# Gating unit 0 alone, and moving the decay rows and the output stores to other DMA issuers, in a fused gated-recurrence and feed-forward kernel

## The chip, the cores and the metric

The kernel runs on one core of a Trainium2 chip. The metric is the device time of one execution in microseconds (us). Where two kernels are compared, a ratio with a 95% interval is given; how it is computed is said with the result. Time points in the text ("at 64.3") count from the first instruction of the profiled execution.

## The reference, cut to what matters

```python
# q, k, v, a_re, a_im: (4 batch, 8 heads, 768 steps, 48), float32
mag   = sqrt(a_re**2 + a_im**2)
scale = minimum(mag, 0.999) / (mag + 1e-6)       # a = (a_re + i a_im) * scale
for t in range(S):                               # S is a complex 48x48 state per head
    S = a[t][:, None] * S + outer(k[t], v[t])
    y[t] = q[t] @ real(S)
x = y as (3072 tokens, 384)
out = x + sigmoid(x @ w_res) * ((gelu(x @ w_gate) * (x @ w_val)) @ w_out)   # 384 -> 1536 -> 384
```

The kernel does not step through time. It takes 256 steps of one batch as a *group* (12 groups, two chunks of 128 steps each), and two groups as a *unit* (6 units, numbered 0 to 5). Within a group the products of decays become exponentials of cumulative sums of log|a| (tiles `E`, `Ei`) and sines of cumulative angles (`fg`, then `CS`), and attention runs on TensorE. Between groups a 96x384 state `G` is carried and multiplied by a decay `M`. `M` comes from rows that lie along one partition and are needed down the partitions: they are turned by writing them to DRAM and reading them back element by element. I call these the turned rows. A *ring* below is the DMA queue of one issuing engine. A *completion semaphore* is a counter that a DMA raises when it has landed and on which other instructions wait.

## The kernel before: what the change and the argument touch

ScalarE needs three function tables in turn: logarithm and exponential (the gate of the next unit), arctangent and sine, and Gelu (the feed-forward). So the work goes in phases. Phase X of unit u holds the rest of its attention, the exponentials of unit u+1, the logarithms of unit u+2 and the sines; phase Y holds the feed-forward of unit u and the first attention of unit u+1.

```python
    def load_q(g):
        for nm, src in (("q", q), ("k", k)):
            ...                                            # nc.sync.dma_start, one per chunk
        t = ldv.tile([128, C, H, D], BF, tag="v", name="v")
        for c in range(C):
            nc.gpsimd.dma_start(out=t[:, c], in_=rows(v, g, c))
    ...
    def turn(nm, g, srcs):                                 # rows to DRAM and back, turned
        n = len(srcs)
        md = dr.tile([n, DM], FP, tag="d" + nm, name="d" + nm)
        for i, src in enumerate(srcs):
            nc.gpsimd.dma_start(out=md[i:i + 1, :], in_=src)
        m = mp.tile([128, n, H], FP, tag=nm, name=nm)
        for u in range(2):
            nc.gpsimd.dma_start(out=m[u * D:(u + 1) * D].rearrange("p r h -> p (r h)"),
                                in_=md.rearrange("r (h d) -> d (r h)", h=H))
        T[nm, g] = m
    ...
    def decay3(g):                                         # M, placed behind the sines
        m = T["m2", g]
        M = mp.tile([128, H], FP, tag="M", name="M")
        nc.vector.tensor_tensor(out=M[0:DD], in0=m[0:DD, 0], in1=m[0:DD, 1], op=OP.mult)
        nc.vector.tensor_tensor(out=M[0:DD], in0=M[0:DD], in1=T["m1", g][0:DD, 0], op=OP.mult)
    ...
        def enter():                                       # attention of a group, first step
            ...
            nc.vector.tensor_tensor(out=G[0:DD], in0=G[0:DD], in1=Mb, op=OP.mult)   # needs M
    ...
    # cs_t: the folding of the angles that the sines need
        r = pS.tile([128, H, D], FP, tag="r", name="r")
        nc.vector.tensor_scalar(out=r, in0=cs3, scalar1=MAGIC, scalar2=MAGIC, op0=OP.add, op1=OP.subtract)
        nc.vector.tensor_tensor(out=fg[:, hs, 1, :], in0=cs3, in1=r, op=OP.subtract)
    ...
    # start: a of units 0 and 1 first, and both are gated in the first phase
    for g in gs(0) + gs(1):
        load_a(g)
    for g in gs(0):
        load_q(g)
    after_landing(T["k", 0], load_w_in)
    ...
        nc.sync.dma_start(out=out[t0:t0 + 128, :], in_=ot)
```

A scheduler orders each engine's instructions from the program's order and priorities. Each engine runs its own list in order.

## Time and profile before

The median was 344.27 us in three runs (342.91 to 344.88); the profiled execution spans 341.4 us.

| part of the span | us | what bounds it |
|---|---|---|
| start to the load of the first Gelu table | 0 to 94.0 | loads, ScalarE's chain, waits for turned rows |
| four units, Gelu table to Gelu table | 94.0 to 278.6 (46.8, 46.4, 47.3, 44.0) | TensorE |
| last unit and the end | 278.6 to 341.4 | TensorE |

The next lines are from the timeline of ScalarE, kernel before. In all views ACT is ScalarE, DVE VectorE, PE TensorE, POOL GpSimd and SP SyncE; a q behind the name marks a DMA that the engine only issues. The columns are start, duration, engine, source line, operation, output<-input, shapes and count; the brackets give how long the engine stood idle before it and what released it. A line with `x2` holds two instructions.

```profile
25.18 0.84 ACT L119 ACTIVATE ar<-ar 128x768 f32<-128x768 f32 x1
29.41 0.84 ACT L119 ACTIVATE ar<-ar 128x768 f32<-128x768 f32 x1 [3.38 <-DMA ar<-in_a_re_dram]
...
35.30 1.28 ACT L445 ACT_TABLE_LOAD   x1
...
64.32 0.21 ACT L119 ACTIVATE m_268<-m_268 96x8 f32<-96x8 f32 x1 [8.90 <-DMA m_268<-dm_266]
...
94.02 1.28 ACT L445 ACT_TABLE_LOAD   x1
...
95.90 1.08 ACT L119 ACTIVATE h_776<-gp 128x512 bf16<-128x512 f32 x2
```

Unit 0's exponentials are done at 25.2, but its trigonometric table is loaded only at 35.3, because unit 1's logarithms stand between. Later ScalarE stops 8.9 us for a turned row. The first Gelu is at 95.9. From there a unit takes about 46 us.

VectorE too stops once for a turned row, as its view of waits shows (line waited on, releaser, total us, times, longest):

```profile
DVE M L273 <- DMA m_247<-dm_244: 4.2, 1, 4.2
```

### The profile page before, as it was taken

To read this page: it belongs to the slowest core of one execution; us is meant where nothing else is said; L and a number is where in the kernel's file an instruction comes from. 1 tells how busy PE (TensorE), PEld (TensorE's weight loads), DVE (VectorE), ACT (ScalarE), POOL (GpSimd) and SP (SyncE) were. 2 spreads that over 40 slices of the span, in tenths; PEclk is the share of its full clock that TensorE was granted. 3 is DMA by queue.
4 is the path that set the end of the run, shared out by engine and by line. 5 is a ranking of instruction groups with operands and counts; after the bars stand their busy time and mean duration, and the time that the engine had idled before them with its cause. 6 is when DMAs were issued, how large, how long until landed. Compare 5 with 4: busy or idle time off the path is not lost.

```text
span 341.4 us, 5552 instructions
## 1 busy us (share of the span) xinstructions
PE 267.3 (78%) x2054; PEld 160.6 (47%) x2080; DVE 245.4 (72%) x440; ACT 203.0 (59%) x338; POOL 67.1 (20%) x104
## 2 busy tenths in 40 slices
PE   0330544298689979899897999779999989999995
PEld 0110224275256545465554566445665556565452
DVE  1322696249999649999389998499994799855443
ACT  3365434349665696756896656977568275662530
POOL 9423710050522224102232000150001300000000
PEclk9996585559699999999999999999999999999999
DMA  9999999999999999527422620021000210002002
GB/s 139 136 139 175 176 184 196 175 170 171 155 167 162 169 133 172 109 46 72 25 63 54 118 46 2 2 48 47 3 2 1 50 46 2 0 2 92 2 1 92
DMA packets 135258, 30.25 MB, mean 89 GB/s; under 512 B 127168, under 2 KB 135232, under 8 KB 135232
## 3 DMA queue, kind: packets, MB, share of 16 engines
q1 hardware_dynamic: 103296, 23.60, 40.6%
q0 software_dynamic: 31936, 6.31, 21.9%
q8 instruction: 16, 0.26, 0.3%
q14 instruction: 10, 0.08, 0.1%
HBM read 31.33 MB, written 4.76 MB: 106 GB/s over the span
## 4 chain that ended last, share of the span: by engine, by line
PE 47%; DMA 18%; DVE 15%; ACT 9%; issue 7%; POOL 3%; ACTq 0%; DVEq 0%; POOLq 0%
PE vp L414 12%; PE gp L410 11%; PE op L434 6%; DMA dm_266<-ar 4%; DMA v<-in_v_dram 4%; PE tp L320 3%; PE at L327 3%; PE tp L317 3%; PE rp L426 3%; DMA dm_663<-Ei 2%; ACT L445 2%; DVE fg L237 2%; DVE r L234 2%; DMA dm_219<-ar 2%; ACT CS L119 2%
## 5 line engine op out<-in xcount | busy, mean ns | idle before, releaser
L410 PE MATMUL gp<-xT,wg 128*128 128x512 bf16 x196 | 61.5, 382 | 7.6 <-DVE xT L401 4.6
L414 PE MATMUL vp<-xT,wv 128*128 128x512 bf16 x210 | 60.3, 382 | 0.3
L322 ACT COPY qk<-tp 96x512 bf16<-96x512 bf16 x48 | 27.9, 581 | 28.3 <-PE tp L320 15.1
L180 DVE TENSOR_TENSOR ai<-s,ai 128x768 f32<-128x768 f32 x12 | 11.1, 955 | 38.5 <-ACT s L119 26.9
L330 DVE TENSOR_TENSOR atm<-at,mask_81 128x512 bf16<-128x512 f32 x48 | 32.8, 683 | 7.2 <-PE at L327 7.2
L410 PEld LDWEIGHTS <-wg 128*128 128x128 bf16 x216 | 20.0, 98 | 23.0 <-issue 8.9
L317 PE MATMUL tp<-ident,Q 128*96 128x128 bf16 x192 | 20.1, 231 | 13.4 <-DVE qk L323 8.6
L142 POOL DMA_DIRECT2D v<-in_v_dram x24 | 21.3, 902 | 43.0 <-PE y L367 22.4
L414 PEld LDWEIGHTS <-wv 128*128 128x128 bf16 x216 | 20.4, 98 | 19.3 <-issue 0.8
L317 PEld LDWEIGHTS <-Q 128*96 128x96 bf16 x192 | 17.3, 131 | 21.4 <-issue 10.0
L323 DVE COPY qk<-tp 96x512 bf16<-96x512 bf16 x48 | 19.9, 414 | 10.1 <-ACT qk L322 9.6
L203 PE MATMUL csl<-ar,lt0a 128*128 128x384 f32 x24 | 12.3, 601 | 18.6 <-DVE ar L189 18.5
L119 ACT ACTIVATE CS<-fg,hpi 128x768 bf16<-128x768 f32 x12 | 11.2, 935 | 24.1 <-DVE fg L237 24.1
L445 ACT ACT_TABLE_LOAD x18 | 23.1, 1283 | 1.0 <-PEq L547 0.7
L320 PE MATMUL tp<-ident,K 128*96 128x128 bf16 x192 | 22.1, 235 | 0.0
L227 PE MATMUL cst<-ai,lt0b 128*128 128x384 f32 x24 | 11.6, 568 | 13.4 <-ACT ai L119 13.1
L327 PE MATMUL at<-qk 96*128 96x128 bf16 x192 | 20.4, 228 | 0.1
L437 DVE SCALAR_TENSOR_TENSOR ot<-sg,op 128x384 f32<-128x384 f32 x24 | 13.2, 549 | 9.4 <-PE op L434 9.4
L365 PE MATMUL y<-v,atm 128*128 128x48 bf16 x192 | 17.9, 187 | 2.5 <-DVE atm L330 2.4
L365 PEld LDWEIGHTS <-atm 128*128 128x128 bf16 x192 | 13.5, 98 | 12.8 <-DVE atm L330 11.6
L320 PEld LDWEIGHTS <-K 128*96 128x96 bf16 x192 | 17.3, 133 | 0.0
L357 PEld LDWEIGHTS <-K 128*96 128x96 bf16 x160 | 13.3, 138 | 6.5 <-DVE K L292 4.2
(155 smaller groups left out, 626.3 us busy)
## 6 DMA issues: line engine op xcount, KB each, us to landing
ar<-in_a_re_dram SPq DMA_DIRECT2D x24, 192.0 KB, 5.7
ai<-in_a_im_dram SPq DMA_DIRECT2D x24, 192.0 KB, 5.5
q<-in_q_dram SPq DMA_DIRECT2D x24, 192.0 KB, 5.1
k<-in_k_dram SPq DMA_DIRECT2D x24, 192.0 KB, 5.0
out_dram<-ot SPq DMA_DIRECT2D x24, 192.0 KB, 1.9
v<-in_v_dram POOLq DMA_DIRECT2D x24, 96.0 KB, 6.3
wg<-in_moe_w_gate_dram POOLq DMA_DIRECT2D x4, 288.0 KB, 9.2
wv<-in_moe_w_val_dram POOLq DMA_DIRECT2D x4, 288.0 KB, 10.5
```

The source lines that it names most:

```text
L142: nc.gpsimd.dma_start(out=t[:, c], in_=rows(v, g, c))
L317: nc.tensor.transpose(out=tp[0:DD, j * 128:j * 128 + 128], in_=Q(x), identity=ident)
L320: nc.tensor.transpose(out=tp[0:DD, 512 + j * 128:640 + j * 128], in_=K(x), identity=ident)
L322: nc.scalar.copy(out=qk[0:DD, 0:512], in_=tp[0:DD, 0:512])
L323: nc.vector.tensor_copy(out=qk[0:DD, 512:1024], in_=tp[0:DD, 512:1024])
L327: nc.tensor.matmul(out=at[:, j], lhsT=qk[0:DD, 512 + j * 128:640 + j * 128], rhs=qk[0:DD, j * 128:j * 128 + 128], start=True, stop=True)
L330: nc.vector.tensor_tensor(out=atm, in0=at, in1=mask4, op=OP.mult)
L365: nc.tensor.matmul(out=ys, lhsT=st["atm", hg][:, j], rhs=V(h), start=True, stop=first)
L410: nc.tensor.matmul(out=gp, lhsT=wg[:, fi, ffi * 128:(ffi + 1) * 128], rhs=xT[:, fi, :], start=(fi == 0), stop=(fi == KD - 1))
L414: nc.tensor.matmul(out=vp, lhsT=wv[:, fi, ffi * 128:(ffi + 1) * 128], rhs=xT[:, fi, :], start=(fi == 0), stop=(fi == KD - 1))
L434: nc.tensor.matmul(out=ps, lhsT=h2[:, ffi, jj * 128:(jj + 1) * 128], rhs=wo[:, ffi, :], start=(ffi == 0), stop=(ffi == KF - 1))
L445: tab(nc.scalar.preload_act_table_set(nm))
```

## The change

The intent: unit 0 is gated alone, so that its sines and its attention come sooner; unit 1's logarithms move into the next phase. q, k and v of unit 0 are loaded ahead of unit 1's a. The turned rows leave GpSimd's DMA queue, in which they stood behind weights, for a queue of ScalarE's own; three rows go in one turn, and `M` is computed on GpSimd. In exchange GpSimd issues the output stores.

```diff
+    def decay_rows(g):
+        er = pS.tile([1, DM], FP, tag="r", name="er")
+        act(out=er, in_=T["lm", g][0:1, 0:DM], func=AF.Exp)
+        md = dr.tile([3, DM], FP, tag="md", name="md")
+        for i, src in enumerate((T["E", g - 1][127:128, DM:W], T["Ei", g][0:1, 0:DM], er)):
+            nc.scalar.dma_start(out=md[i:i + 1, :], in_=src)
+    def decay(g):
+        m = mp.tile([128, 3, H], FP, tag="m", name="m")
         for u in range(2):
-            nc.gpsimd.dma_start(...)
+            nc.scalar.dma_start(out=m[u * D:(u + 1) * D].rearrange("p r h -> p (r h)"),
+                                in_=T["md", g].rearrange("r (h d) -> d (r h)", h=H))
         M = mp.tile([128, H], FP, tag="M", name="M")
-        nc.vector.tensor_tensor(out=M[0:DD], ...)                  # two of them
+        nc.gpsimd.tensor_tensor(out=M[0:DD], ...)                  # two of them
...
-        nc.sync.dma_start(out=out[t0:t0 + 128, :], in_=ot)
+        nc.gpsimd.dma_start(out=out[t0:t0 + 128, :], in_=ot)
...      # phase_x, u < 0: p1 of unit 0 only, then rows, table, arctangent, decay, fold, sines
+        if u == 0:
+            first = [st for g in g1 for st in p1_steps(g)]
+            weave((0.0, 0.3, first), (0.3, 0.4, csls), (0.4, 0.6, exs), (0.4, 0.7, p1),
+                  (0.7, 0.75, [trig] + [call(p1_arctan, g) for g in g1]), (0.72, 0.72, dec), (0.75, 0.9, cst),
+                  (0.9, 1.0, sin + atn), (0.0, 0.8, att))
+            return
...
-    for g in gs(0) + gs(1):
+    for g in gs(0):
         load_a(g)
     for g in gs(0):
         load_q(g)
-    after_landing(T["k", 0], load_w_in)
+        load_v(g)
+    for g in gs(1):
+        load_a(g)
+    after_landing(T["ai", 2], load_w_in)
+    for g in gs(1):
+        load_q(g)
...      # u == -1
-            for g in gs(1):
-                load_q(g)
-            after_landing(T["k", 2], load_w_out)
+            after_landing(T["q", 2], lambda: [load_v(g) for g in gs(1)])
+            after_landing(T["q", 3], load_w_out)
```

More of the change, by code (lines that the diff above doesn't have):

```diff
@@ L139, in load_q, with load_v @@
             T[nm, g] = t
+    def load_v(g):
         t = ldv.tile([128, C, H, D], BF, tag="v", name="v")
@@ L245, in p2_sin @@
         act(out=T["CS", g][:, :, 1], in_=T["fg", g][:, :, 1], func=AF.Sin, scale=2.0 * math.pi)
-    def turn(nm, g, srcs):
-        n = len(srcs)
-        md = dr.tile([n, DM], FP, tag="d" + nm, name="d" + nm)
-        for i, src in enumerate(srcs):
-            nc.gpsimd.dma_start(out=md[i:i + 1, :], in_=src)
-        m = mp.tile([128, n, H], FP, tag=nm, name=nm)
-        for u in range(2):
-            nc.gpsimd.dma_start(out=m[u * D:(u + 1) * D].rearrange("p r h -> p (r h)"),
-                                in_=md.rearrange("r (h d) -> d (r h)", h=H))
-        T[nm, g] = m
-    def decay0(g):
-        turn("m1", g, [T["lm", g][0:1, 0:DM]])
-    def decay1(g):
-        m = T["m1", g]
-        act(out=m[0:DD], in_=m[0:DD], func=AF.Exp)
-    def decay2(g):
-        turn("m2", g, [T["E", g - 1][127:128, DM:W], T["Ei", g][0:1, 0:DM]])
-    def decay3(g):
-        m = T["m2", g]
+    def decay_rows(g):
[4 more added lines that the diff above has]
+            nc.scalar.dma_start(out=md[i:i + 1, :], in_=src)
+        T["md", g] = md
+    def decay(g):
+        m = mp.tile([128, 3, H], FP, tag="m", name="m")
+        for u in range(2):
+            nc.scalar.dma_start(out=m[u * D:(u + 1) * D].rearrange("p r h -> p (r h)"),
+                                in_=T["md", g].rearrange("r (h d) -> d (r h)", h=H))
         M = mp.tile([128, H], FP, tag="M", name="M")
-        nc.vector.tensor_tensor(out=M[0:DD], in0=m[0:DD, 0], in1=m[0:DD, 1], op=OP.mult)
-        nc.vector.tensor_tensor(out=M[0:DD], in0=M[0:DD], in1=T["m1", g][0:DD, 0], op=OP.mult)
+        nc.gpsimd.tensor_tensor(out=M[0:DD], in0=m[0:DD, 0], in1=m[0:DD, 1], op=OP.mult)
+        nc.gpsimd.tensor_tensor(out=M[0:DD], in0=M[0:DD], in1=m[0:DD, 2], op=OP.mult)
         T["M", g] = M
@@ L472, in phase_x @@
         d1 = [g for g in g1 if g % NS > 0]
-        d2 = [g for g in g2 if g % NS > 0]
         ops = [call(op_step, u - 1, jj) for jj in range(4)] if 0 <= u - 1 < NU else []
@@ L484, in ex @@
             pend.pop(0)()
-        def p1(g):
-            return p1_steps(g) + ([call(decay0, g)] if g % NS > 0 else [])
         csls = [call(csl, g, c) for g in g1 for c in range(C)]
-        exs = [ex for _ in g1 for _ in range(C)]
-        dec = [call(decay2, g) for g in d1]
-        atn = [table("trig_and_small")] + [call(p1_arctan, g) for g in g2]
+        exs = [ex for _ in g1 for _ in range(C)] + [call(decay_rows, g) for g in d1]
+        dec = [call(decay, g) for g in d1]
         cst = [call(carry, g) for g in g1] + [call(cs_t, g, c) for g in g1 for c in range(C)]
         sin = [call(p2_sin, g) for g in g1]
-        dec1 = [call(decay1, g) for g in d1]
-        dec3 = [call(decay3, g) for g in d1]
+        trig = table("trig_and_small")
         table("natural_log_exp_and_others")()
         if u < 0:
-            for f in [st for g in g1 for st in p1(g)] + csls + exs + dec + zip_steps([p1(g) for g in g2]) + dec1:
-                f()
-            for f in atn[:1] + [call(p1_arctan, g) for g in g1] + cst + sin + atn[1:] + dec3:
+            for f in ([st for g in g1 for st in p1_steps(g)] + csls + exs + [trig]
+                      + [call(p1_arctan, g) for g in g1] + dec + cst + sin):
                 f()
             return
-        weave((0.0, 0.12, csls), (0.05, 0.5, zip_steps([p1(g) for g in g2])), (0.01, 0.01, dec1), (0.12, 0.45, exs),
-              (0.46, 0.46, dec), (0.2, 0.65, cst), (0.7, 0.95, atn + sin), (0.95, 0.95, dec3), (0.0, 0.8, att), (0.1, 1.0, ops))
+        atn = [call(p1_arctan, g) for g in g2]
+        p1 = zip_steps([p1_steps(g) for g in g2])
+        if u == 0:
[4 more added lines that the diff above has]
+            return
+        weave((0.0, 0.12, csls), (0.05, 0.5, p1), (0.12, 0.45, exs), (0.46, 0.46, dec), (0.2, 0.65, cst),
+              (0.7, 0.95, [trig] + atn + sin), (0.0, 0.8, att), (0.1, 1.0, ops))
     def phase_y(u):
@@ L532 @@
             load_q(g)
+            load_v(g)
 _INS = ['q', 'k', 'v', 'a_re', 'a_im', 'moe_w_gate', 'moe_w_val', 'moe_w_out', 'moe_w_res']
```

## The prediction

> **What bounds the kernel now.** From 96 us on, the timeline shows a steady 46 us per unit (feed-forwards start at about 96, 142, 188, 234, 280). There TensorE is busy 41 of 46 us at full granted clock (table by windows): near a compute floor, 245 of the 341.4 us. The first 96 us are start-up: TensorE is busy about 42 us, often at half clock, and the page's DMA row is full. Unit 0's exponentials are ready at 25.2 us, but its arctangent starts at 36.6: in between ScalarE waits for and works on unit 1's a. Attention starts at 48.2; at 55.4 ScalarE stops for 8.9 us for a turned decay row (waits view: m_268), because that row took 13.9 us in GpSimd's queue behind the weights. VectorE waits 4.2 us for another (m_247).
>
> **What the change does.**
> 1. Unit 0 is gated alone and its q, k, v come ahead of unit 1's a; 4 instead of 12 v loads compete at the start. ai of group 1, awaited until 17.1 us, should land at 13 to 16. The trigonometric table load comes at about 24 instead of 35.3, attention at 32 to 37 instead of 48.
> 2. The 8.9 and 4.2 us waits for turned rows go.
> 3. Unit 1's first pass is not removed, it moves into the next phase. I count about 43 us of ScalarE work between unit 0's first sine and the first Gelu; if ScalarE is 80 to 90% busy, the first Gelu comes at 78 to 87 us instead of 96. DMA can bind here: unit 2's a now comes behind unit 1's q and k and beside the weights; from the trace's rates (one 192 KB load per us alone, half that beside weights) it lands near 60 us, just in time or some us late.
> 4. Given back: ScalarE gets, per decay (8), a one-row exponential (0.49 us), three small DMA issues and two of 1,152 elements. SyncE needs 0.5 us to issue 1,024 rows when quiet; I estimate 2 us of ScalarE per decay, plus waits for the round trip. In the gate phases ScalarE is packed until its second table load, then idles 2 to 3 us for VectorE; so 2 to 4 us in all, 8 if its issues block.
> 5. Stores by GpSimd: 0.5 to 0.9 us per issue in the trace, against 0.36 on SyncE, on an idle engine; about 1 us at the tail. The Trainium skill ("DMA: Bandwidth & Descriptors", Issuing engines are not separate dma queues) says all issuing engines share the same 16 DMA engines; so I expect the own ring to cure the queueing of item 2, not to add bandwidth. The trace agrees: loads slow down beside weights.
>
> **Critical path and time.** Start-up gains 9 to 18 us, about 15; items 4 and 5 take back about 4. Predicted 333 us, range 326 to 341. Chances: faster 0.76, same 0.20, slower 0.04.
>
> **What would show it.** Step 1: table load near 24 us, first attention matmul before 38. Step 2: no multi-microsecond ScalarE or VectorE wait on a turned row. Step 3: first Gelu at 78 to 87. Step 4: later units 46 to 48 us apart. Step 5: under 4 us from the last VectorE result to the end.
>
> **What would make it wrong.** ScalarE's issues blocking for microseconds while the DMA engines are full, or its in-order wait for the round trip; unit 2's a or unit 1's v landing late, so that the first feed-forward starts near 92 anyway; GpSimd's queue holding M or the weights behind waiting loads; TensorE at half clock in the first feed-forward.

## The result, and the profile after

The kernel after the change takes 362.37 us (median of 4 runs, 361.9 to 363.14) against 343.59 us of the kernel before in the same rounds (342.57 to 344.88). The ratio is 1.0547, interval 1.0502 to 1.0592: slower by 5.5%. A ratio here is the mean time of one kernel's fast runs over the mean of the other's fast runs of the same rounds, so it is not quite the ratio of the medians that I quote.

From the timeline of TensorE, kernel after, its first attention matmul:

```profile
32.66 0.42 PE L309 MATMUL tp<-ident,Q 128*96 128x128 bf16 x4 [2.44 <-DVE Q L284]
```

From the timeline of ScalarE, kernel after. ACTq lines are DMAs that ScalarE issues:

```profile
22.23 1.28 ACT L437 ACT_TABLE_LOAD   x1 [0.28 <-ACT er L119]
...
60.60 0.84 ACT L119 ACTIVATE ar<-ar 128x768 f32<-128x768 f32 x1 [3.90 <-DMA ar<-in_a_re_dram]
...
74.67 0.84 ACT L119 ACTIVATE ar<-ar 128x768 f32<-128x768 f32 x1 [12.09 <-DMA ar<-in_a_re_dram]
...
79.84 0.51 ACT L119 ACTIVATE er<-ar 1x384 f32<-1x384 f32 x1
83.53 0.24 ACTq L256 DMA_DIRECT2D md<-Ei  x1
85.13 0.22 ACTq L256 DMA_DIRECT2D md<-er  x1
85.48 0.84 ACT L119 ACTIVATE s<-ai 128x768 f32<-128x768 f32 x1 [5.13 <-DMA k<-in_k_dram]
...
88.18 1.28 ACT L437 ACT_TABLE_LOAD   x1
89.30 1.11 ACTq L262 DMA_DIRECT2D m<-md  x2
...
99.98 0.94 ACT L119 ACTIVATE CS<-fg,hpi 128x768 bf16<-128x768 f32 x1 [7.95 <-DVE fg L239]
...
107.94 1.28 ACT L437 ACT_TABLE_LOAD   x1
109.23 1.09 ACT L119 ACTIVATE h_762<-gp 128x512 bf16<-128x512 f32 x2
```

And VectorE in the same stretch:

```profile
91.92 0.56 DVE L219 TENSOR_TENSOR P<-P 128x384 f32<-128x384 f32 x1
95.55 0.56 DVE L336 TENSOR_TENSOR G<-G,M 96x384 f32<-96x384 f32 x1 [3.07 <-POOL M L266]
...
98.99 0.95 DVE L239 SCALAR_TENSOR_TENSOR fg<-fg 128x768 f32<-128x768 f32 x1
```

What to see. The start does what was intended: the trigonometric table comes at 22.2 instead of 35.3, attention starts at 32.7 instead of 48.2. But the first Gelu comes at 109.2 instead of 95.9. Between lie two waits for unit 2's a (16.0 us together), a 5.1 us stop that is put down to a load of k, which `s<-ai` does not read, and a multiplication of `G` by `M` that stands in VectorE's list ahead of the folding of unit 1's angles. The table by windows shows how empty that stretch is. The columns are the window, its length, then busy time of TensorE, weight loads, VectorE, ScalarE and GpSimd, the granted clock, the DMA share and GB/s. The kernel before:

```profile
62.00:82.00 20.00, 14.97 (x131) 11.68 (x131) 11.22 (x20) 11.75 (x23) 4.73 (x7) 0.65 1.23 169
```

The same window in the kernel after:

```profile
62.00:82.00 20.00, 0.81 (x6) 0.41 (x5) 3.92 (x5) 6.26 (x13) 2.96 (x4) 0.58 1.51 161
```

In the kernel after no engine is busy for even 7 of these 20 us, while the DMA share is higher than before (1.51 against 1.23).

The loss by phase, from the starts of the Gelu table loads in both traces:

| stretch | before | after | difference |
|---|---|---|---|
| start to first Gelu table | 94.0 | 107.9 | +13.9 |
| unit 0 to unit 1 | 46.8 | 49.4 | +2.6 |
| unit 1 to unit 2 | 46.4 | 47.9 | +1.5 |
| unit 2 to unit 3 | 47.3 | 47.2 | -0.1 |
| unit 3 to unit 4 | 44.0 | 42.4 | -1.6 |
| unit 4 to the end | 62.9 | 65.6 | +2.7 |
| sum | 341.4 | 360.5 | +19.1 |

Three quarters of the loss are made before the first Gelu, in the phase from which the gain was to come. The experiments are about that phase, and about the stores.

### The profile page after: what moved, and what is told of

It is laid out like the page before. It is cut to its first block, busy times and chain, and to the rows that moved or that the text cites. A ratio compares the mean times of both kernels' runs of the same rounds, so it can differ in the third digit from the quotient of the medians.

```text
span 360.5 us, 5508 instructions
## 1 busy us (share of the span) xinstructions
PE 274.7 (76%) x2052; PEld 165.4 (46%) x2080; DVE 246.1 (68%) x424; ACT 206.7 (57%) x338; POOL 51.6 (14%) x89
## 4 chain that ended last, share of the span: by engine, by line
PE 31%; issue 20%; DMA 14%; DVE 13%; SPq 13%; ACT 6%; POOL 2%; ACTq 1%; POOLq 0%; DVEq 0%
PE vp L406 8%; PE gp L402 8%; SPq L138 7%; SPq L131 6%; DMA m<-md 6%; DMA ar<-in_a_re_dram 5%; PE tp L312 2%; PE tp L309 2%; PE at L319 2%; PE rp L418 2%; PE op L426 2%; DVE r L236 2%; DMA ai<-in_a_im_dram 2%; ACT L437 1%; PE dk L349 1%
## 5 line engine op out<-in xcount | busy, mean ns | idle before, releaser
L402 PE MATMUL gp<-xT,wg 128*128 128x512 bf16 x196 | 60.0, 381 | 2.2 <-DVE fg L237 0.9
L432 POOL DMA_DIRECT2D out_dram<-ot x24 | 13.2, 550 | 168.2 <-DVE ot L430 160.8
L182 DVE TENSOR_TENSOR ai<-s,ai 128x768 f32<-128x768 f32 x12 | 11.4, 954 | 23.6 <-ACT s L119 16.6
L272 DVE TENSOR_TENSOR qE<-q,E 128x768 bf16<-128x768 f32 x12 | 11.4, 952 | 20.3 <-ACT E L119 20.3
L309 PEld LDWEIGHTS <-Q 128*96 128x96 bf16 x192 | 18.2, 135 | 15.1 <-issue 5.6
L312 PE MATMUL tp<-ident,K 128*96 128x128 bf16 x192 | 22.9, 241 | 0.0
L387 PE MATMUL tpx<-ident,x 128*128 128x128 bf16 x72 | 8.9, 233 | 16.9 <-ACT Ei L119 14.1
L119 ACT ACTIVATE ar<-ar 128x768 f32<-128x768 f32 x12 | 9.8, 839 | 20.1 <-DMA ar<-in_a_re_dram 20.1
L429 DVE SCALAR_TENSOR_TENSOR ot<-sg,op 128x384 f32<-128x384 f32 x24 | 13.2, 550 | 11.6 <-PE op L426 11.6
```

Source lines behind the costliest of these rows:

```text
L119: tab(nc.scalar.activation(**kw))
L309: nc.tensor.transpose(out=tp[0:DD, j * 128:j * 128 + 128], in_=Q(x), identity=ident)
L312: nc.tensor.transpose(out=tp[0:DD, 512 + j * 128:640 + j * 128], in_=K(x), identity=ident)
L402: nc.tensor.matmul(out=gp, lhsT=wg[:, fi, ffi * 128:(ffi + 1) * 128], rhs=xT[:, fi, :], start=(fi == 0), stop=(fi == KD - 1))
```

## The experiments

Three readings of the trace compete.

- **L, late loads.** Unit 2's a now comes behind unit 1's q and k and beside the weights, and its 16 us of waits are the loss.
- **D, DMA engines full.** The rows are slow because the engines are full, whoever issues them; where the rows are issued does not matter.
- **Q, ScalarE's issues are blocked.** ScalarE cannot issue a row's DMA while certain loads of SyncE's are under way (which ones is shown under a_best), and, being in order, stops all work behind it.

A fourth, **M, a late M blocks VectorE**, came out of the first results. In the expectations of the first runs, R is the rival from which Q came, and S is that the stores cost the time. The table gives all runs in the order in which they are told. The kernel before is at 343.3 to 344.1 us in all of these rounds.

| kernel | what it is | median us | ratio to before, 95% interval | first Gelu at |
|---|---|---|---|---|
| before | | 343.59 | 1 | 95.9 |
| after | the whole change | 362.37 | 1.0547 [1.0502, 1.0592] | 109.2 |
| b_stores | before, stores by GpSimd | 347.08 | 1.0122 [1.0078, 1.0165] | 95.4 |
| a_stores | after, stores by SyncE | 359.31 | 1.0443 [1.0376, 1.0511] | 108.7 |
| b_decay | before, rows on ScalarE's ring | 357.93 | 1.0427 [1.0372, 1.0483] | 105.8 |
| a_decay | after, rows on GpSimd's ring | 369.22 | 1.0721 [1.0650, 1.0793] | 111.8 |
| a_a2first | after, unit 2's v and w_out behind unit 2's a | 365.43 | 1.0641 [1.0609, 1.0673] | 112.0 |
| a_best | after, unit 2's a ahead of unit 1's q, k and all weights | 363.86 | 1.0585 [1.0558, 1.0613] | 110.4 |
| a_hold | a_best, SyncE's next loads held until M is there | 343.99 | 1.0003 [0.9943, 1.0064] | 90.8 |
| a_best_pool | a_best, rows on GpSimd's ring | 368.03 | 1.0698 [1.0642, 1.0753] | 105.7 |
| a_best_pool_k | a_best_pool, G behind the products | 357.18 | 1.0379 [1.0344, 1.0415] | 99.9 |
| a_best_pool_k_er | a_best_pool_k, er in its own buffer | 355.96 | 1.0319 [1.0268, 1.0370] | 101.3 |
| a_hold_k | a_hold, G behind the products | 342.25 | 0.9946 [0.9909, 0.9982] | 87.2 |
| a_hold_k_st | a_hold_k, stores by SyncE | 338.42 | 0.9840 [0.9809, 0.9871] | 88.0 |
| a_hold_k_st_er | a_hold_k_st, er in its own buffer | 339.41 | 0.9842 [0.9800, 0.9885] | 87.3 |

All gave correct results.

### b_stores and a_stores: the stores alone

```diff
-        nc.sync.dma_start(out=out[t0:t0 + 128, :], in_=ot)      # b_stores, on the kernel before
+        nc.gpsimd.dma_start(out=out[t0:t0 + 128, :], in_=ot)
```

a_stores is the reverse edit on the kernel after.

> The kernel before, with only the output stores moved from SyncE to GpSimd. Theory L (late loads: the change lost its time because unit 2's a landed at 75 us, behind unit 1's q and k and beside the weights, v and w_out on GpSimd's queue, and ScalarE's in-order queue held unit 1 behind it): the stores cost at most 2 us, 341 to 346 us. Rival S (stores on GpSimd's queue cost the time): 350 or more.

> The changed kernel, with only the output stores back on SyncE. The stores alone cost 3.8 us on top of the kernel before; if that adds up, 356 to 360 us; if their cost was hidden here by other waits, 361 to 364.

Moving the stores costs 1.2% on the kernel before (3.8 us between the medians, more than the 2 us expected), and moving them back gains about 1% on the kernel after (1.0547 to 1.0443). The cost is at the very end. The last result and the last store, from the timeline of the kernel before, which ends at 341.4:

```profile
338.10 0.56 DVE L438 TENSOR_TENSOR ot<-ot,x 128x384 f32<-128x384 f32 x1
338.68 0.33 SPq L440 DMA_DIRECT2D out_dram<-ot  x1
```

And from the timeline of b_stores, which ends at 344.2:

```profile
337.77 0.56 DVE L438 TENSOR_TENSOR ot<-ot,x 128x384 f32<-128x384 f32 x1
338.62 0.54 POOL L440 DMA_DIRECT2D out_dram<-ot  x1 [1.41 <-DVE ot L438]
```

From the end of VectorE's last instruction to the end of the program it is 2.8 us with SyncE and 5.9 us with GpSimd, though GpSimd starts the issue only 0.3 us after VectorE is done, against 0.02 us on SyncE. The landing is not the difference either: the last store lands 2.2 us after its issue in b_stores and 1.9 us in the kernel before. But in b_stores GpSimd's closing DRAIN instruction ends 2.3 us after that landing (1.4 us in the kernel after). In the kernel after the whole stretch is 4.7 us, in a_stores 2.8. The stores are a small, additive loss at the tail.

### b_decay and a_decay: the rows' issuer alone

```diff
-            nc.gpsimd.dma_start(...)     # b_decay: both DMAs of turn(), on the kernel before
+            nc.scalar.dma_start(...)
```

a_decay is the reverse edit on the kernel after.

> The kernel before, with only the DMAs of the turned decay rows issued by ScalarE instead of GpSimd, in the old places. Theory L: the 8.9 us ScalarE wait near 55 us goes or shrinks, the issues cost ScalarE 1 to 2 us per decay; in all 336 to 348 us. Rival R (ScalarE's blocking DMA issues and the round trip cost the time): 352 or more.

> The changed kernel, with only the DMAs of the decay rows issued by GpSimd again. Theory Q (found in the last runs: ScalarE's and SyncE's DMAs share 8 completion semaphores, handed out in turn; a ScalarE issue waits until the SyncE load that used its semaphore before has landed, and ScalarE computes nothing meanwhile): ScalarE's 5.1 us wait before the row issues goes, but unit 2's a still lands late (12.1 us wait), so 352 to 360 us. Theory L (late loads alone): within 2 us of the changed kernel, 360 to 365.

With nothing else of the change, issuing the rows from ScalarE, on its ring, costs the kernel before 4.3%. In b_decay, ScalarE and VectorE both stand for a turned row. The view of waits for ScalarE:

```profile
ACT xT L399 <- DMA m<-dm: 19.7, 4, 12.1
```

The view of waits for VectorE, b_decay:

```profile
DVE M L273 <- DMA m<-dm: 11.0, 3, 8.7
```

`xT` is a copy that has nothing to do with the row; it stands behind the row's DMA in ScalarE's list. That is against D as it was put: the same bytes on the same busy engines cost more because ScalarE issues them. But giving the rows back to GpSimd in the kernel after (a_decay) made it slower, not faster, and there VectorE stands for `M`, which is then late in GpSimd's queue. The view of waits for VectorE, a_decay:

```profile
DVE G L336 <- POOL M L266: 27.7, 2, 26.2
```

So either way of issuing loses in the new order of work. The expectation for a_decay failed on this second wait; it is followed up below.

### a_a2first and a_best: take the late loads away

```diff
 # a_a2first
-            after_landing(T["q", 3], load_w_out)
+            after_landing(T["ai", 5], load_w_out)
 ...
+        if u == -1:
+            after_landing(T["ai", 5], lambda: [load_v(g) for g in gs(2)])
```

```diff
 # a_best
     for g in gs(1):
         load_a(g)
-    after_landing(T["ai", 2], load_w_in)
+    for g in gs(2):
+        load_a(g)
+    after_landing(T["ai", 5], load_w_in)
     for g in gs(1):
         load_q(g)
```

> The changed kernel, with only w_out and unit 2's v held back until unit 2's a has landed. Theory L: unit 2's last a lands 8 to 15 us earlier, ScalarE's 12.1 us wait for it shrinks by that, and the whole run takes 347 to 355 us. Rivals R and S: 359 or more, since neither ring nor stores are touched.

> The changed kernel, with unit 2's a issued ahead of unit 1's q and k and the weights of the first layer held until it has landed; the order of instructions on ScalarE is the same. Theory L: unit 2's a lands by about 42 us, ScalarE does not wait for it, the first Gelu comes at 78 to 88 us instead of 109, and the run takes 330 to 341 us. Rivals R and S: 357 or more.

Late loads alone do not explain the time. In a_a2first ScalarE's waits for unit 2's a shrink from 3.9 and 12.1 us to 5.4 and 2.3, but it then stands 9.5 us before the issue of `m<-md`, and the time is no better. In a_best the waits of 3.9 and 12.1 us for unit 2's a are gone and ScalarE's order of instructions is the same, yet the time is no better. The timeline of ScalarE, a_best, shows what took their place:

```profile
64.01 0.51 ACT L119 ACTIVATE er<-ar 1x384 f32<-1x384 f32 x1
67.13 0.24 ACTq L256 DMA_DIRECT2D md<-Ei  x1
72.51 0.22 ACTq L256 DMA_DIRECT2D md<-er  x1
72.86 0.84 ACT L119 ACTIVATE s<-ai 128x768 f32<-128x768 f32 x1 [8.34 <-DMA k<-in_k_dram]
...
85.17 2.51 ACTq L262 DMA_DIRECT2D m<-md  x2
87.73 1.58 ACT L119 ACTIVATE ai<-ai 128x768 f32<-128x768 f32 x2 [10.89 <-DMA ar<-in_a_re_dram]
...
100.61 0.94 ACT L119 ACTIVATE CS<-fg,hpi 128x768 bf16<-128x768 f32 x1 [11.30 <-DVE fg L239]
```

`er`, the last row, is ready at 64.5. The issue of `md<-Ei`, which is next in the list, starts at 67.1, that of `md<-er` at 72.5, and that of `m<-md` at 85.2. Each issue takes a quarter of a microsecond or so by its record; the time is lost ahead of it. The view names loads of k and a that these instructions do not read. The Trainium skill ("Perfetto Trace Analysis", DMA Instruction — HWDGE (DVE, Sync)) says why the record looks short: the start that the profiler reports is the moment at which all semaphores are satisfied. And "DMA: Bandwidth & Descriptors" (Anatomy of one DMA — SWDGE (gpsimd) path) says of DMAs in general that a semaphore wait happens on the issuing sequencer. This trace agrees: ScalarE does nothing from 64.5 to 67.1, then issues in 0.24 us.

Which semaphore? I read the semaphore records of the trace by hand. In this program as built, the DMAs of SyncE and of ScalarE complete on the same eight semaphores, handed out in turn in the order of the schedule; GpSimd's DMAs have eight others. For each of ScalarE's row DMAs of this phase I compared the moment it could have started with the last update of its own completion semaphore, made by an earlier load of SyncE's:

```
a_best     could start   its semaphore's last update, by        issued at
md<-Ei         64.52     67.11  SyncE's load of q, issued 54.20   67.13
md<-er         67.36     72.44  SyncE's load of k, issued 60.20   72.51
m<-md          77.15     85.11  SyncE's load of k, issued 76.06   85.17
m<-md (2nd)    85.50     87.34  SyncE's load of a, issued 78.56   87.36
```

Each issue follows the landing of an unrelated load by 0.02 to 0.07 us. In these runs no DMA of ScalarE's was issued before the earlier DMA on its semaphore had landed. Summed over the whole execution (an issue within 0.12 us of such a landing, and the gap ahead of it, counted from when ScalarE was free and its other waits were over), these gaps are 19.6 us in a_best, 18.9 in b_decay (the largest 8.6, from 81.4 to 90.0) and 6.2 in the kernel after. In the kernel after they are small, as I read it, because ScalarE already stands 16 us for unit 2's a while the loads land. That fits what a_best showed: with one wait removed, the other took its place. So the late loads are not cleared of a part: all versions below that gain load unit 2's a first, and no run holds the loads back without that.

### a_hold: no load under way when the rows are issued

```diff
+    def hold(t, held):
+        if held is not None:
+            nc.gpsimd.tensor_copy(out=t[0:1, :, 0, 0], in_=T["M", held][0:1, 0:C])
...  # a_best, and:
+        if u == 0:
+            for g in gs(2):
+                load_q(g, 2)
-        for g in gs(u + 3) if u > -1 else []:
-            load_a(g)
+        for g in gs(u + 3) if u > -1 else []:
+            load_a(g, 2 if u == 0 else None)
...  # load_q of unit 2 at its old place is dropped
```

A tiny copy from `M` into the tile of each following load makes the load wait until `M` of the first phase is done. The load overwrites it.

> The changed kernel with unit 2's a first, as in the run a_best, and SyncE's loads of unit 2's q and k and unit 3's a held back until unit 1's decay is there; ScalarE's order is unchanged and GpSimd's weights and v still keep the DMA engines busy. Theory Q: with no load in flight on the shared semaphores ScalarE issues its rows at once (a_best: gaps of 2.6, 5.2, 8.3 and 1.9 us shrink to under 0.5 each), the first Gelu comes at 80 to 92 us, and the run takes 335 to 348 us. Rival D (the DMA engines are simply full, rows take 8 us or more whoever issues): the waits stay, 355 or more.

It took 343.99 us; the ratio to the kernel before falls from a_best's 1.0585 to 1.0003. From the timeline of ScalarE, a_hold:

```profile
63.42 0.51 ACT L119 ACTIVATE er<-ar 1x384 f32<-1x384 f32 x1
63.95 0.22 ACTq L263 DMA_DIRECT2D md<-er  x1
...
68.53 1.50 ACTq L269 DMA_DIRECT2D m<-md  x2
...
81.54 0.94 ACT L119 ACTIVATE CS<-fg,hpi 128x768 bf16<-128x768 f32 x1 [9.88 <-DVE fg L246]
...
90.80 1.09 ACT L119 ACTIVATE h<-gp 128x512 bf16<-128x512 f32 x2
```

`md<-er` is issued 0.03 us after `er` is done (8.0 us in a_best), `m<-md` at 68.5 instead of 85.2, and the first Gelu is at 90.8 instead of 110.4. The blocked issues sum to 1.5 us. This edit also takes load traffic out of the phase, so by itself it does not separate Q from D. The next one does.

### a_best_pool: the same loads, the rows on the other set of semaphores

```diff
-            nc.scalar.dma_start(...)     # both DMAs of the rows, on a_best
+            nc.gpsimd.dma_start(...)
```

> The run a_best with only the DMAs of the decay rows issued by GpSimd, whose DMAs have other completion semaphores than SyncE's. Theory Q: ScalarE no longer stands before its row issues; the rows themselves are late behind v, so the first Gelu comes at 85 to 97 us, 338 to 352 us in all. Rival D: 357 or more.

The loads are those of a_best. ScalarE's blocked issues are gone, since it issues nothing. Its timeline, a_best_pool:

```profile
67.29 1.28 ACT L437 ACT_TABLE_LOAD   x1
68.59 1.58 ACT L119 ACTIVATE ai<-ai 128x768 f32<-128x768 f32 x2
98.74 0.94 ACT L119 ACTIVATE CS<-fg,hpi 128x768 bf16<-128x768 f32 x1 [28.58 <-DVE fg L239]
```

Both arctangents (`ai<-ai`) are done at 70.2, where a_best ends them at 89.3. So with the same traffic ScalarE runs free when its list holds no row DMA: Q holds against D for ScalarE. But the time did not fall, and my expectation failed. ScalarE waits 28.6 us for the folding, and VectorE shows why (a_best_pool):

```profile
70.06 0.56 DVE L219 TENSOR_TENSOR P<-P 128x384 f32<-128x384 f32 x1
94.23 0.56 DVE L336 TENSOR_TENSOR G<-G,M 96x384 f32<-96x384 f32 x1 [23.62 <-POOL M L266]
```

The scheduler placed the multiplication of `G` by `M` ahead of the folding of unit 1's angles. `M` is done only at 94.2, because its rows stand in GpSimd's queue behind v and w_out. VectorE stands, and with it the sines, though neither the folding nor the sines need `M`. In the kernel before the same multiplication stood behind the folding, at 93.17.

### a_best_pool_k and a_hold_k: M made harmless by order alone

```diff
-                nc.vector.tensor_tensor(out=t, in0=T["CS", g], in1=sb, op=OP.mult)       # products Q, K
+                T[nm + "i", g] = nc.vector.tensor_tensor(out=t, in0=T["CS", g], in1=sb, op=OP.mult)
...
-                nc.vector.tensor_tensor(out=G[0:DD], in0=G[0:DD], in1=Mb, op=OP.mult)
+                i = nc.vector.tensor_tensor(out=G[0:DD], in0=G[0:DD], in1=Mb, op=OP.mult)
+                tc.add_manual_dep(i.ins, T["Ki", g].ins.name, order, reason="G after K")
```

The added edge is one of order on VectorE only. No wait is taken away.

> a_best_pool with one order edge: the multiplication of G by M stands behind the K product of its group on VectorE, so behind the folding (fg) that unit 1's sines need. Theory (a late M blocks VectorE's queue): the ScalarE wait for fg, 28.6 us in a_best_pool, falls below 6 us, unit 1's sines are done by about 80 us, the first Gelu comes at 80 to 95 instead of 105.7, and VectorE still waits for M until about 94 us, now behind the products, so that only part comes back: 353 to 363 us. Rival (the late rows or the full DMA engines hold the kernel in another way): first Gelu after 102 and the time within 1 per cent of 368.

> a_hold with the same order edge. The 5.0 us that VectorE waits for M (it landed at 76.6 us) leaves the path of unit 1's sines: ScalarE's wait for fg falls from 9.9 to about 4 us, the first Gelu comes at 85 to 89 instead of 90.8, and the time is 338 to 343 us. If M is needed at once behind the products all the same, the time stays at 344.

a_best_pool_k gains 10.9 us on a_best_pool between their medians, within the expected range. `G` now waits 2.3 us for `M` instead of 23.6. But only half of what was written down held: the wait for the folding fell from 28.6 to 17.5 us, not below 6, and the first Gelu came at 99.9, not by 95. The timeline of VectorE, a_best_pool_k, has a wait that I had not seen coming:

```profile
85.66 0.56 DVE L236 TENSOR_SCALAR r<-cst 128x384 f32<-128x384 f32 x1 [11.56 <-DMA md<-er]
```

`r`, the scratch tile of the folding, waits for the row's DMA to have read `er`: the change puts `er` into the same pair of buffers (`tag="r"`), so a row whose DMA is slow holds a buffer that VectorE needs. This DMA was issued at 72.1 on GpSimd's ring and had landed only at 85.6, 13.5 us later. In a_best the same row, issued at 72.5 on ScalarE's ring beside the same kind of traffic, had landed at 77.1.

In a_hold_k, where `M` lands early enough, the first Gelu (87.2 instead of 90.8) and the time are as expected. ScalarE's wait for the folding falls less than expected, from 9.9 to 7.4 us and not to about 4. ScalarE's timeline, a_hold_k:

```profile
77.78 0.94 ACT L119 ACTIVATE CS<-fg,hpi 128x768 bf16<-128x768 f32 x1 [7.36 <-DVE fg L246]
...
87.20 0.60 ACT L119 ACTIVATE h<-gp 128x512 bf16<-128x512 f32 x1
```

In VectorE's timeline of a_hold_k, `G` no longer waits for anything:

```profile
82.10 0.55 DVE L343 TENSOR_TENSOR G<-G,M 96x384 f32<-96x384 f32 x1
```

The gain in time, 343.99 to 342.25 us, comes from different rounds; against the kernel before the ratio goes from 1.0003 to 0.9946.

### a_best_pool_k_er: the shared buffer alone

```diff
-        er = pS.tile([1, DM], FP, tag="r", name="er")
+        er = pK.tile([1, DM], FP, tag="er", name="er")
```

> a_best_pool_k with the row er in a buffer of its own instead of one of the two that the folding's r uses. Theory (the change couples VectorE to the row's DMA through that shared buffer: r waited 11.6 us for md<-er to land): this wait is gone, unit 1's first sine starts at 74 to 80 us instead of 88.2, and VectorE then stands 8 to 18 us for M at G, because M still lands near 94; the first Gelu comes at 84 to 99 and the time is 350 to 357 us (a_best_pool_k: 357.2). If the buffer has no part in it, the first sine stays at 88.

The wait for the buffer is gone and the first sine comes at 75.9 instead of 88.2, as the theory asks. From ScalarE's timeline, a_best_pool_k_er:

```profile
75.92 0.94 ACT L119 ACTIVATE CS<-fg,hpi 128x768 bf16<-128x768 f32 x1 [7.20 <-DVE fg L239]
...
99.38 0.58 ACT L314 COPY qk<-tp 96x512 bf16<-96x512 bf16 x1 [16.18 <-PE tp L312]
```

And from VectorE's, a_best_pool_k_er:

```profile
96.25 0.56 DVE L336 TENSOR_TENSOR G<-G,M 96x384 f32<-96x384 f32 x1 [15.93 <-POOL M L266]
```

But VectorE then stands 15.9 us at `G` until `M` is there, everything behind it in its list with it, and the first Gelu is at 101.3 (99.9 with the shared buffer), later than I had expected. The time, 355.96 against 357.18 us, hardly moves. So the shared buffer was a real wait, and not the last one: two waits, one behind the other, hang on the same slow row. In this branch neither edit brings the first Gelu below 99 us, as long as `M` is there only near 95.

### a_hold_k_st and a_hold_k_st_er: a version that beats both kernels

a_hold_k_st is a_hold_k with the stores on SyncE again; a_hold_k_st_er gives `er` its own buffer besides.

> a_hold_k with the output stores back on SyncE, everything else the same: 2 to 3 us under a_hold_k of the same rounds, 335 to 341 us, if the stores' cost (3.1 us between the last VectorE instruction and the end, seen with the stores alone moved) adds up; the end of the kernel is 2.7 us after the last VectorE instruction instead of about 5. If the stores' semaphores on SyncE hold up ScalarE's rows as the loads' did, the gain is smaller or gone.

> a_hold_k_st with the row er in a buffer of its own. There the waits through that buffer are small (2.2 us of a ScalarE activation for md<-er, 2.1 us of er for fg): 335.5 to 338.5 us against 338.4; no more than 3 us are in it, and nothing if these waits are covered by others.

a_hold_k_st takes 338.42 us, ratio 0.984 to the kernel before, interval 0.9809 to 0.9871: the best version, 1.6% under the kernel before (the interval leaves out 1) and about 6.6% under the kernel after (338.42 over 362.37). The stores' gain adds up, 3.8 us between medians of the same rounds where 2 to 3 were expected, and the end is 2.8 us after VectorE's last instruction again (4.7 in a_hold_k). The own buffer for `er` gave nothing there: 0.9842 against 0.984, and its 339.41 us lie just outside the range expected.

## Why the prediction was wrong

I predicted 333 us, faster, and the kernel took 362. Point by point:

1. **Unit 0 alone (item 1): right.** Table load predicted at about 24, measured 22.2; attention predicted at 32 to 37, measured 32.7.
2. **"The 8.9 and 4.2 us waits for turned rows go" (item 2), with "the own ring to cure the queueing" (item 5): this is the step that failed.** The queueing itself was cured: a row took 1.1 to 4.7 us from issue to landing on ScalarE's ring (after, a_best and b_decay), against 13.9 us for the awaited row in the kernel before. But the ring is not independent of SyncE: both draw on the same completion semaphores, so a row is issued only when an unrelated load has landed, and ScalarE stands meanwhile with all its work behind. b_decay shows that the change of issuer alone costs 4.3%, with 18.9 us of such stops; a_hold and a_best_pool show that the stop goes when no load of SyncE's is under way, or when ScalarE issues no rows.
3. **"The first Gelu comes at 78 to 87 us" (item 3): wrong by 22 us or more; measured 109.2.** I had named late loads as the risk and put unit 2's a near 60. It was worked on at 60.6 and 74.7, so "some us late" was 16. By itself this was not the cause of the time: with that wait gone (a_best) nothing was gained, since the blocked issues came in its place. The term of the estimate that failed is the busy share. The busy times of all engines between unit 0's first sine and the first Gelu (columns as above), kernel after:

```profile
29.56:109.23 79.67, 35.61 (x267) 24.49 (x266) 44.68 (x72) 37.51 (x57) 22.03 (x31) 0.66 1.31 171
```

And in a_hold_k:

```profile
30.24:87.20 56.96, 32.00 (x266) 22.50 (x265) 44.08 (x71) 37.26 (x56) 22.57 (x39) 0.75 1.45 181
```

ScalarE's work is 37.5 and 37.3 us, less than the 43 counted. But it was busy 47% of the stretch and not 80 to 90%, and still only 65% in a_hold_k, without the late loads, with hardly any blocked issues and with `M` out of VectorE's way. There the first Gelu comes at 87.2, just past the range.
4. **"2 to 4 us in all, 8 if its issues block" (item 4): mis-sized.** The issues do block, by up to 8.6 us for one DMA; 19.6 us in all in a_best and 18.9 in b_decay. I had costed the issue and not the wait ahead of it, and I had only listed "ScalarE's issues blocking for microseconds" as a risk. A chance of 0.04 for slower was far too small for a risk that I could name.
5. **What I did not see:** the moved `M`. In the kernel before `M` was multiplied into `G` behind the folding. In the new order this multiplication stands ahead of it in VectorE's list, so a late row stops VectorE too: 3.1 us in the kernel after, 6.4 in a_best, 23.6 in a_best_pool. The new `er` also shares buffers with the folding, a wait of 11.6 us where the row was slow (a_best_pool_k).
6. **Stores (item 5): about 1 us predicted, about 3 measured** (3.1 us at the end of b_stores, from 2.8 to 5.9; 1.2% of its time). "Under 4 us from the last VectorE result to the end" was 4.7.
7. **Units 46 to 48 us apart (step 4):** 49.4, 47.9, 47.2 and 42.4; only the middle two are in the range. In a_hold_k the first two units still take 1.9 and 1.2 us more than before, and I did not find out why; this stays open.

So a start-up gain was there to be had, but a smaller one than the 9 to 18 us predicted. Late loads, blocked issues and a late `M` ate it, each covering for the others, and it appears when all three are taken away: 94.0 to 85.9 for the first Gelu table in a_hold_k, 8.1 us. The span of that execution is only 3.8 us shorter (337.6 against 341.4), and it is the fastest of six; between the medians of its rounds the gain is 1.5 us. So in it 4.3 us were given back later: 1.9 and 1.2 us in the first two units, 0.0 and -1.5 in the next two, and 2.7 in the last stretch, of which 1.9 lie behind VectorE's last instruction (4.7 against 2.8), where the stores are.

What is not settled: no run gives ScalarE's DMAs completion semaphores of their own, so the coupling is shown by the semaphore records and by two edits that avoid it, not by removing it alone. How the loss divides between late loads, blocked issues and `M` is not shown, and fewer, larger loads were not tried.

## What to carry to other kernels

Before DMAs are put on a compute engine's own ring, look at what they will wait for ahead of their issue, above all which earlier DMAs share their completion semaphores, because an in-order engine stops with everything behind them. A short DMA record says nothing of that wait; look for an idle stretch that is put down to a load which the next instruction does not read. And when a small late value (here `M`, 96x8) feeds a long in-order list, place its consumer behind everything that does not need it, and give its source no buffer that others wait for: moving or removing only the first of several waits on the same late value gains little. Last, an estimate of work over busy share is only as good as the share: here it was 47% and at the best 65%, where 80 to 90% had been assumed.

## What the Trainium skill lacked or had wrong

- "DMA: Bandwidth & Descriptors", Issuing engines are not separate DMA queues: the page says that issuing from several engines will "only save the time on the sequencer it takes to initiate the DMA". The runs show that it can also cost: rows issued by ScalarE made the kernel before 4.3% slower, with 18.9 us of blocked issues (b_decay), where the record of an issue is 0.2 to 0.9 us.
- No page that I found gives the cost in time when the DMAs of two issuing engines are given the same completion semaphores, as in this program: a DMA is then not issued until the earlier one on its semaphore has landed (issued 0.02 to 0.07 us after that landing in the four cases shown of a_best; 19.6 us of gaps in all). Whether this is so in other programs no run here shows.
- "Perfetto Trace Analysis", DMA Instruction — HWDGE (DVE, Sync): it is right that the reported start is after the semaphore wait, and the trace agrees (0.24 us reported, 2.6 us of standing ahead of it). What it does not tell is that the semaphore waited for can be shared with an unrelated DMA, so that the gap (8.3 us ahead of `s<-ai` in a_best) is put down to a load that is no operand.
- "DMA: Bandwidth & Descriptors", Queues, rings and completion order: it says that each DMA engine takes turns between the queues it has work for, packet by packet. This fits a 1.5 KB row landing in 4.6 us on ScalarE's ring (a_best) and in 13.5 us on GpSimd's (a_best_pool_k), in which v and w_out stood ahead of it. The page gives no such figure, and no run here separates the ring from the issuer.
- No page that I found gives what a last store by GpSimd costs at the end of a program: from VectorE's last instruction to the end 4.15 to 5.9 us in ten runs, against 2.8 to 3.3 us with SyncE in five, a part of it in GpSimd's closing DRAIN instruction (it ends 2.3 us after the store has landed in b_stores, 1.4 us in the kernel after).
